# Spectral filter and two-layer MLP in one kernel: first-stage pieces every second tick, transforms done by tick 148, three more blocks by Strassen's scheme

## The chip, the cores and the metric

The kernel runs on one core of a Trainium2 chip. The metric is the device time of one execution, in microseconds (us). Before the change the median of 3 runs is 1342.98 us (1342.41 to 1349.44).

## The reference

Everything is fp32. `x` has 4 batches of 3008 rows of 256; the MLP has 12032 tokens, 256 inputs and 2048 hidden values.

```python
X = np.fft.rfft(x, axis=1)                      # 4 x 1505 x 256
Yr = Xr @ w_r - Xi @ w_i + b_r
Yi = Xr @ w_i + Xi @ w_r + b_i
Yr = sign(Yr) * max(|Yr| - 0.01, 0)             # the same for Yi
x = irfft(Yr + 1j * Yi, n=3008).reshape(12032, 256)
h = x @ w_in                                    # 256 -> 2048
g = h / (1 + exp(-h))
out = g @ w_out                                 # 2048 -> 256
```

## The kernel before

**Precision.** Most products split both factors into a high and a low part of TensorE's faster fp32 format and issue three matmuls: high times high, low times high, high times low. A split is a copy on ScalarE (the high part) and a subtraction on VectorE (the low part).

**The transforms** are matrix products in stages of 47 and 64 points, with the layout between the stages changed by a store to device memory and a load. For batches 1 to 3:
- The *first stage* of batches 2 and 3 comes in 16 *pieces* a batch. `stack_split` splits a piece of the input, `stack_product` multiplies it (two matmuls of 512 columns, lines 287 to 300, one PSUM bank each; ScalarE copies one half of the rows out, VectorE adds it to the other) and stores it; it then asks for the input of the piece after the next one (`x_ahead`, on POOL's queue).
- The *second stage* has 12 units a batch. In a *step* `u3_step(b, u, 0)`, `s2_3` does the second transform of unit u (8 small matmuls in one bank, "s2"), `split_z` splits the shrunk spectrum of unit u-2, and `i1` does the first inverse stage of unit u-3 (6 matmuls, another bank). In a *mix* `u3_step(b, u, 1)`, `mix3` multiplies unit u-1 by the weights (18 matmuls of 256 columns: 6 in a first bank, 12 in a second). ScalarE, POOL and VectorE then add bias and shrink; the VectorE part (`shrink`) is put on the list `deferred`.
- The *last stage* `i2(i, 0)`, `i2(i, 1)`, `i2_ends(i)` makes the 512 tokens of MLP block i, already transposed, in three products; `i2_load` loads what they read.

**The MLP** works on 24 blocks of 512 tokens (the last has 256). A block has 16 *ticks*, one for each 128 hidden values. In an ordinary tick `mlp1` does six matmuls of 512 columns (the first layer) and ScalarE applies the activation; `split_g` splits the result in the next tick; `mlp2` does the second layer of the tick before the last one: four groups of a 512- and a 256-column matmul into four accumulators. Blocks in `FAST` do the first layer by Strassen's scheme: in a pair of ticks, seven products of 2 x 2 blocks instead of eight, 21 matmuls of 256 columns instead of 12 of 512, with more additions on VectorE and POOL, and with sums of the weights (`fast_weights`) and of the tokens (`fast_moving`) made beforehand.

**PSUM.** Of eight banks, four are the second layer's accumulators, two ("h") the first layer's, and two ("d0", "d1") are handed out in turn by `bank(name)` (line 175) to every product of the transforms. A bank is written again only when those that read it are done.

**The order of work** is written out by hand. `ticks` lists (block, f); `fill[t]` holds what a tick t does besides. A loop at the end (lines 1085 to 1119) issues, for each tick: the deferred shrinks, `split_g` of the tick before, `mlp1`, then `fills(t)`, then the second layer with `run`. `fills` ends with `flush`, which issues up to four waiting stores on SP's queue. `put(t, ...)` (line 1002) takes the next tick that is free; ticks 33, 49, 65, ... are kept free, since the outputs of a block are copied out there. Before the change every last-stage product, every piece and every step or mix has a tick of its own, by the strings of "U" (a step or a mix) and "S" (a piece); the transforms end with tick 183, and blocks 13 to 22 are in `FAST`.

Of the kernel before, what the change touches and what calls it, by code (L numbers as in the profile page):

```python
# [9 lines left out]
F32 = mybir.dt.float32  # L10
# [23 lines left out]

STACKED = 2

FAST = range(13, 23)

X_BUFS = [0, 1, 2, 3, 4, 5, 6, 0, 1, 2, 3, 4, 0, 2, 1, 0]
BLOCKS = [(c, min(BLK, NT - c)) for c in range(0, NT, BLK)]  # L40
# [109 lines left out]
def spectral_mlp_kernel(ctx: ExitStack, tc: tile.TileContext, x, w_r, w_i, b_r, b_i, w_in, w_out, c1, c2, c3, c4, c3f, c5, out):  # L150
# [24 lines left out]
    def bank(name):  # L175

        state["d"] += 1
        tag, bufs = f"d{state['d'] % 2}", 1
        if state["prologue"]:
            tag, bufs = ((f"d{state['d'] // 4 % 2}", 1), ("acc", 4), ("h", 2), ("acc", 4))[state["d"] % 4]  # L180
        if state["fast"]:
            tag = "d1"
        return ps.tile([128, 512], F32, tag=tag, bufs=bufs, name=name)
# [10 lines left out]
    def flush(n):  # L194
        for dst, src in stores[:n]:
            nc.sync.dma_start(out=dst, in_=src)
        del stores[:n]
# [280 lines left out]
    def pieces(c0, n):  # L478

        c = c0  # L480
        while c < c0 + n:
            b, q = divmod(c, S)
            v = next(v for v in PLACES[b] if v[0] <= q < v[0] + v[1])
            p0 = q - v[0]
            m = min(v[1] - p0, c0 + n - c)
            yield c - c0, b, v, p0, m
            c += m
# [11 lines left out]
            nc.sync.dma_start(out=t[0:96, q], in_=v[:, j * D:(j + 2) * D])  # L499
            nc.sync.dma_start(out=t[96:120, q], in_=w[h * NR:(h + 1) * NR, c * D:(c + 2) * D])  # L500

    def i2_load(i):
        if i >= len(BLOCKS):
            return
        for _, b, (_, _, kind, k), _, _ in pieces(*BLOCKS[i]):
            g = k // 4 if kind == "pair" else ("five", k[0] // 2)
            if (b, g) not in loaded:
                loaded.add((b, g))
                if kind == "five":
                    f_load(b, g[1])  # L510
                else:
                    g_load(b, g, cols=slice(k % 4 * D, 4 * D))
# [4 lines left out]
    def i2_columns(p, e, b, place):  # L517
# [9 lines left out]
        for h, o in enumerate((0, NP)):  # L527
# [3 lines left out]
                start=(h == 0), stop=(h == 1), skip_group_check=True,  # L531
            )

    def i2(i, e):

        c0, n = BLOCKS[i]
        if e == 0:
            v = "ab"[i > 0] if i < 3 else "ab"[(i + 1) % 2]
            xt[i] = tuple(sb.tile([128, 2, BLK], F32R, tag=f"xt{v}{k}", bufs=1, name=f"xt{k}") for k in range(2))
        whole = [v for v in pieces(c0, n) if v[4] == v[2][1]]  # L540
        p = bank("i2")
        for o, b, place, _, m in whole:
            i2_columns(p[:, o:o + m], e, b, place)
        q = slice(whole[0][0], whole[-1][0] + whole[-1][4])
        if i in FAST and e == 0:
            xf[i] = tl.tile([128, 2, BLK], F32, tag="xf", bufs=1, name="xf")
        split_x(i, p[:, q], (slice(None), e, q))
# [9 lines left out]
    def i2_ends(i):  # L557

        c0, n = BLOCKS[i]
        if i in rest:  # L560
            t = rest.pop(i)
            split_x(i, t, (slice(None), slice(None), slice(0, t.shape[-1])))
        o, b, place, p0, m = list(pieces(c0, n))[-1]
        z = place[1]
        if p0 == 0 and m < z:
            p = bank("i2e").rearrange("p (e c) -> p e c", e=2)[:, :, :z]
            for e in range(2):
                i2_columns(p[:, e, :], e, b, place)
            split_x(i, p[:, :, 0:m], (slice(None), slice(None), slice(o, o + m)))
            rest[i + 1] = sb.tile([128, 2, 216], F32, tag="rest", bufs=1, name="rest")[:, :, 0:z - m]  # L570
            nc.scalar.copy(rest[i + 1], p[:, :, m:z])
# [63 lines left out]
    def fast_moving(i):  # L635

        x32 = xf.pop(i)
        d = tl.tile([128, 4, HB], F32, tag="td", bufs=1, name="td")
        hi = tl.tile([128, 4, HB], F32R, tag="th", bufs=2, name="th")
        lo = tl.tile([128, 4, HB], F32R, tag="tl", bufs=2, name="tl")  # L640
        th[i] = (hi, lo)
        l0, r0, l1, r1 = x32[:, 0, 0:HB], x32[:, 0, HB:BLK], x32[:, 1, 0:HB], x32[:, 1, HB:BLK]

        def low(k):
            nc.gpsimd.tensor_sub(lo[:, k, :], d[:, k, :], hi[:, k, :])

        nc.gpsimd.tensor_sub(d[:, 0, :], r0, l0)
        yield
        nc.gpsimd.tensor_sub(d[:, 1, :], r1, d[:, 0, :])
        yield  # L650
        nc.gpsimd.tensor_sub(d[:, 2, :], r1, r0)
        nc.scalar.copy(hi[:, 0:2, :], d[:, 0:2, :])
        yield
        low(0)
        yield
        nc.gpsimd.tensor_sub(d[:, 3, :], l1, d[:, 1, :])
        yield
        low(1)
        nc.scalar.copy(hi[:, 2:4, :], d[:, 2:4, :])
        yield  # L660
        low(2)
        yield
        low(3)
# [176 lines left out]
    with tc.manual_schedule():  # L840
# [156 lines left out]
        def at(t, fn, *args):  # L997
            fill.setdefault(t, []).append((fn, args))
# [3 lines left out]
        def put(t, fn, *args):  # L1002

            while t in taken:
                t += 1
            taken.add(t)
            at(t, fn, *args)
            return t

        for i in range(1, len(BLOCKS)):  # L1010
            t = (16 * i - 15 if i in FAST else 16 * i - 9) if i > 1 else -1
            if i > 1:
                at(t, i2_load, i)
            put(t + 2, i2, i, 0)
            put(t + 4, i2, i, 1)
            t = put(t + 6, i2_ends, i)
            if i in FAST:
                moving = fast_moving(i)
                for k in range(8):
                    at(t + 1 + k, next, moving, None)  # L1020
                assert t + 8 < 16 * i
        for t, n in enumerate(W_GO):
            at(t, w_go, n)
        at(0, x_ahead)
# [5 lines left out]
        m3 = mix3_weights()  # L1030
        for t in (16, 22, 23):
            at(t, next, m3, None)
        def turns(b):

            for u in range(NU + 3):
                for half in range(2 if 0 < u <= NU else 1):
                    yield b, u, half

        free, stacked = 24, 18
        for b, order in ((1, "U" * 4 + "UUUUSUUUS" * 3 + "UU" + "S." * 10), (2, "UUSUUSUSUS" * 3 + "USUS" + "USU" * 2 + "UUU"), (3, "U" * 27)):  # L1040
            todo, split = list(turns(b)), 0
            assert order.count("U") == len(todo) and order.count("S") in (0, 16)
            ready = max(free, stacked + 4)
            for k in range(2):
                at(ready - 2 + k, u_load, b, k)
            for k in order:
                if k == "U":
                    free = put(max(free, ready), u3_step, *todo.pop(0))
                elif k == "S":
                    while free in taken:  # L1050
                        free += 1
                    at(max(free - 2, stacked), stack_split, b + 1, split)
                    stacked = put(free, stack_product, b + 1, split)
                    split += 1
                last = free
                free += 1

        def swap_pools():
            nonlocal tl
# [4 lines left out]
        for q in range(NFF // 2):  # L1064
            steps = fast_weights(q)
            for k in range(3):
                at(last + 2 + q * 8 // 5 + k, next, steps, None)
        assert last + 1 <= 16 * FAST[0] - 13 and last + 2 + 11 + 2 < 16 * FAST[0] + 12

        def fills(t):  # L1070
            for fn, args in fill.pop(t, []):
                fn(*args)
            flush(1 if t < 12 else 4)

        def run(n):
            for v in units[:n]:
                mlp2(*v)
            del units[:n]
# [5 lines left out]
        first_fast, last_fast = 16 * FAST[0], 16 * (FAST[-1] + 1)  # L1084
        for t in range(len(ticks) + 1):
            i, f = ticks[t] if t < len(ticks) else (LAST, None)
            while deferred:
                deferred.pop(0)()
            if t and ticks[t - 1][0] not in FAST:
                split_g(*ticks[t - 1])  # L1090
            if i in FAST:
                q = t - first_fast
                if f % 2 == 0:
                    state["fast"] = True
                    fast_one(i, f // 2)
                    run(2)
                    if q:
                        fast_two()
                        run(2 if q > 2 else 0)
                else:  # L1100
                    fast_more()
                    if f != 3:
                        rest_of_pair()
                    run(2 if q < 4 else 4)
                    rest_of_pair()
                fills(t)
                continue
            if t == last_fast:
                run(2)
                fast_two()  # L1110
                run(3)
                rest_of_pair()
            if f is not None:
                mlp1(i, f)
            fills(t)
            if last_fast <= t < last_fast + 3:
                run(3 if t == last_fast else 4)
            else:
                run(sum(v[:2] != ticks[t - 1] for v in units))
        run(len(units))  # L1120
        for k, (dst, src) in enumerate(stores):
            eng = nc.scalar if k % 2 else nc.sync
# [28 lines left out]
```

## Time and profile before

| | |
|---|---|
| median of 3 runs | 1342.98 us (1342.41 to 1349.44) |
| profiled execution, its own time | 1344.73 us |
| its span, first to last instruction | 1342.9 us |
| granted TensorE clock, mean over the span | 0.997 |
| busy: TensorE matmuls, weight loads | 1328.4 us (99%), 1176.5 us (88%) |
| busy: VectorE, ScalarE, POOL | 857.0 us (64%), 790.3 us (59%), 191.0 us (14%) |
| DMA | 109.96 MB, mean 82 GB/s |

PE is TensorE's matmuls, PEld its weight loads, DVE VectorE, ACT ScalarE, POOL GpSimd and SP SyncE, which issues most DMAs. L591 is line 591 of the kernel before. Matmuls are pipelined and overlap: one of 512 columns is shown with 0.40 us, while the next starts 0.23 us later, so start to start is the measure of a matmul's cost. In the timeline a bracket at the end of a line gives the idle time before it and what ended it.

### The profile page before, as it was taken

Reading aid. Unit: us, or ns where it says so; the run is one execution under the profiler, and the core shown is the slowest. Engines: PE = TensorE matmul, PEld = TensorE weight load, DVE = VectorE, ACT = ScalarE, POOL = GpSimd, SP = SyncE. Lnnn points to the kernel's source line nnn. Section 1 sums busy time; section 2 is a strip of 40 time slices with the busy share of each in tenths; the row PEclk is TensorE's granted clock in tenths of the full one; section 3 lists DMA queues with packets and bytes.
Section 4 is the critical chain, followed back from the end, with each engine's and each line's share of the span. In section 5 each row is a group of like instructions: output and inputs, shape, how many; then the busy total and the mean of one; then the engine's idle time right before and its main releaser. Section 6 shows DMA issues by size and latency. Waiting matters only on the chain.

```text
span 1342.9 us, 22228 instructions
## 1 busy us (share of the span) xinstructions
PE 1328.4 (99%) x8221; PEld 1176.5 (88%) x8221; DVE 857.0 (64%) x1628; ACT 790.3 (59%) x1646; POOL 191.0 (14%) x292
## 2 busy tenths in 40 slices
PE   8989999999999999999999999999999999999998
PEld 4967888888888888888889888899999999999998
DVE  3867747675665757676556557366666666666663
ACT  5546555565676666575555455466656665666555
POOL 2000002111111212120111100211112111211100
PEclk9999999999999999999999999999999999999999
DMA  8875514342345345251424121011001110110000
GB/s 274 261 214 172 151 40 113 95 116 67 101 105 149 93 111 147 70 144 36 141 64 125 53 77 30 2 32 31 16 23 31 31 30 3 31 32 13 4 22 25
DMA packets 76121, 109.96 MB, mean 82 GB/s; under 512 B 8854, under 2 KB 54798, under 8 KB 76014
## 3 DMA queue, kind: packets, MB, share of 16 engines
q1 hardware_dynamic: 61895, 79.17, 20.5%
q0 software_dynamic: 10544, 25.68, 7.4%
q10 hardware_dynamic: 3575, 3.70, 0.9%
q8 instruction: 65, 1.06, 0.3%
q14 instruction: 42, 0.34, 0.1%
HBM read 71.03 MB, written 37.49 MB: 81 GB/s over the span
## 4 chain that ended last, share of the span: by engine, by line
PE 95%; DMA 4%; ACT 1%; DVE 0%; SPq 0%; issue 0%; ACTq 0%; DVEq 0%
PE acc L749 25%; PE h L591 22%; PE h L672 15%; PE acc L753 13%; PE mix L415 6%; PE s L390 2%; PE i L462 2%; PE mix L354 2%; PE i2e L529 2%; PE i L529 2%; PE s L293 1%; DMA scr<-i1o 1%; DMA scr<-s1o 1%; PE acc L744 1%; PE i L459 1%; PE i L522 1%
## 5 line engine op out<-in xcount | busy, mean ns | idle before, releaser
L749 PE MATMUL acc<-wout,gh 128*128 128x512 f32 x1472 | 541.3, 398 | 0.6 <-ACT gh L607 0.6
L753 PE MATMUL acc<-wout,gl 128*128 128x256 f32 x1472 | 413.5, 281 | 0.2 <-DVE gl L608 0.2
L591 PE MATMUL h<-xt,win 128*128 128x512 f32 (+1 forms) x1344 | 339.2, 387 | 0.0
L749 PEld LDWEIGHTS acc<-wout,gh 128*128 128x128 f32 x1472 | 277.9, 189 | 50.1 <-ACT gh L607 0.8
L598 ACT ACTIVATE g<-h 128x512 f32<-128x512 f32 (+2 forms) x225 | 130.9, 582 | 267.4 <-PE h L591 265.3
L753 PEld LDWEIGHTS acc<-wout,gl 128*128 128x128 f32 x1472 | 277.1, 188 | 5.0 <-DVE gl L608 0.5
L591 PEld LDWEIGHTS h<-xt,win 128*128 128x128 f32 x1344 | 232.2, 188 | 48.1 <-DVE xt L555 0.4
L608 DVE TENSOR_TENSOR gl<-g,gh 128x512 fp32r<-128x512 f32 (+2 forms) x225 | 151.2, 674 | 75.8 <-ACT gh L607 73.2
L607 ACT CAST gh<-g 128x512 fp32r<-128x512 f32 (+2 forms) x225 | 136.1, 606 | 1.5
L720 DVE TENSOR_TENSOR gl<-gp,gh 128x512 fp32r<-128x512 f32 x160 | 113.7, 711 | 24.4 <-ACT gh L719 24.4
L710 ACT ACTIVATE gp<-gp 128x256 f32<-128x256 f32 x80 | 33.4, 417 | 135.6 <-DVE gp L707 135.6
L719 ACT CAST gh<-gp 128x512 fp32r<-128x512 f32 x160 | 99.3, 621 | 5.2
L434 DVE TENSOR_TENSOR y<-q,mix 64x256 f32<-64x256 f32 x144 | 60.3, 419 | 59.1 <-PE mix L415 56.8
L422 POOL TENSOR_TENSOR q<-q,bias 128x256 f32<-128x256 f32 x36 | 26.5, 737 | 405.9 <-ACT q L421 405.9
L672 PE MATMUL h<-xt,win 128*128 128x256 f32 x480 | 83.8, 283 | 0.2 <-DVE gp L707 0.2
L712 DVE TENSOR_TENSOR gp<-h,u 128x256 f32<-128x256 f32 x80 | 33.9, 424 | 60.7 <-ACT gp L711 60.7
L672 PEld LDWEIGHTS h<-xt,win 128*128 128x128 f32 x480 | 68.2, 189 | 3.8 <-DVE gp L707 0.4
L672 PE MATMUL h<-th,sw_h 128*128 128x256 f32 x240 | 70.2, 293 | 0.0
L672 PE MATMUL h<-th,sw_l 128*128 128x256 f32 x240 | 68.0, 283 | 0.0
L672 PE MATMUL h<-tl,sw_h 128*128 128x256 f32 x240 | 67.4, 281 | 0.0
L295 DVE TENSOR_TENSOR s1o<-s,s1o 48x512 f32<-48x512 f32 x64 | 41.0, 678 | 32.3 <-ACT s1o L294 32.2
L707 DVE TENSOR_TENSOR gp<-h,u 128x256 f32<-128x256 f32 x80 | 33.8, 423 | 42.7 <-PE h L672 42.4
(175 smaller groups left out, 2260.0 us busy)
## 6 DMA issues: line engine op xcount, KB each, us to landing
a<-scr SPq DMA_DIRECT2D x48, 256.0 KB
x_sb<-in_x_dram POOLq DMA_DIRECT2D x64, 188.0 KB, 3.7
gin<-scr SPq DMA_DIRECT2D x48, 192.0 KB
t<-in_c_dram POOLq DMA_DIRECT2D x36, 256.0 KB, 3.2
scr<-i1o SPq DMA_DIRECT2D x36, 256.0 KB
t<-in_c_dram SPq DMA_DIRECT2D x48, 128.0 KB
scr<-s1o SPq DMA_DIRECT2D x32, 192.0 KB
scr<-s1o SPq DMA_DIRECT2D x13, 384.0 KB
```

The costliest lines, as they stand in the source:

```text
L415: nc.tensor.matmul(out=out, lhsT=x_[:, e, c, :], rhs=m[:, e, :], start=(n == 0), stop=(n == 5))
L434: nc.vector.tensor_tensor(out=y[64 * i:64 * i + 64, r, :], in0=q[rows, i, :], in1=pv[rows, i, :], op=op,)
L529: nc.tensor.matmul(out=p[:, o:o + NP + RR], lhsT=t[:, q:q + 128], rhs=c4_sb[:, h * (NP + RR):(h + 1) * (NP + RR)], start=(h == 0), stop=(h ...
L591: nc.tensor.matmul(out=p[:, :n], lhsT=w[:, e, f * 128:(f + 1) * 128], rhs=v[:, e, :n], start=(m == 0), stop=(m == 5),)
L598: nc.scalar.activation(out=g[:, q], in_=p[:, q], func=ACTF.Silu)
L607: nc.scalar.copy(gh[:, q], g[:, q])
L608: nc.vector.tensor_sub(gl[:, q], g[:, q], gh[:, q])
L672: nc.tensor.matmul(out=p, lhsT=w[j], rhs=m[k], start=(begins and n == 0), stop=(n == 2), skip_group_check=True,)
L719: nc.scalar.copy(h, v)
L720: nc.vector.tensor_sub(l, v, h)
L749: nc.tensor.matmul(out=a, lhsT=gh[:, q], rhs=wout[:, f].rearrange("p a c -> p (a c)"), start=begins, stop=False,)
L753: nc.tensor.matmul(out=a[:, D:2 * D], lhsT=gl[:, q], rhs=wout[:, f, 0, :], start=False, stop=ends,)
```

## The change

`FAST` begins at block 10 instead of 13. The planner of ticks is new:
- Pieces are placed first, at least two ticks apart; steps and mixes take the other ticks, in order. A last-stage product of blocks 3 to 9 no longer has a tick of its own: it joins a tick with a mix or a piece (or, when its time is up, any), at least two ticks after the last one.
- Keys of `fill` may be fractions. `fills(t - 0.25)` and `fills(t - 0.125)` come before the tick's `mlp1`, `fills(t + 0.5)` after its second layer. A mix is put at t - 0.125. A last-stage product that joins a mix or a step is put at t + 0.5; a piece that a last-stage product joins is itself put at t + 0.5, and the split of the next piece at t + 0.75.
- The deferred shrinks are issued after `mlp1` of the mix's own tick, no longer at the start of the next one. `flush` runs in the whole ticks only.
- The last stage takes an "h" bank (`stage_bank`), except in the opening and while Strassen blocks run.
- The load of a batch's first group of columns waits for the third of a block's products (`late`).
- The steps end with tick 148. The weight sums then take ticks 150 to 163, and block 10, the first of `FAST`, starts at tick 160.

The diff, without the parts that only pass `late` on:

```diff
-FAST = range(13, 23)
+FAST = range(10, 23)
...
+    def stage_bank(name):
+
+        if state["prologue"] or state["fast"]:
+            return bank(name)
+        return ps.tile([128, 512], F32, tag="h", bufs=2, name=name)
...
-        p = bank("i2")
+        p = stage_bank("i2")
...
-            p = bank("i2e").rearrange("p (e c) -> p e c", e=2)[:, :, :z]
+            p = stage_bank("i2e").rearrange("p (e c) -> p e c", e=2)[:, :, :z]
...
+        steps = []
+        for b in range(1, NB):
             for u in range(NU + 3):
-                for half in range(2 if 0 < u <= NU else 1):
-                    yield b, u, half
-
-        free, stacked = 24, 18
-        for b, order in ((1, "U" * 4 + "UUUUSUUUS" * 3 + "UU" + "S." * 10), (2, "UUSUUSUSUS" * 3 + "USUS" + "USU" * 2 + "UUU"), (3, "U" * 27)):
...
+                steps.extend((b, u, half) for half in range(2 if 0 < u <= NU else 1))
+        pieces_left = [(b, q) for b in range(STACKED, NB) for q in range(16)]
+        turned = []
+        for i in range(3, FAST[0]):
+            at(16 * i - 15, i2_load, i)
+            begins = any(v[1] and v[2][0] == 0 for v in pieces(*BLOCKS[i]))
+            turned.extend((16 * i - (3 if k == 2 and begins else 13), 16 * i - 7 + 2 * k, fn)
+                          for k, fn in enumerate(((i2, i, 0), (i2, i, 1), (i2_ends, i))))
+        stacked, last, begun = {1: 18}, 24, set()
+        ended = {}
+        done, behind, t, since = 37, False, 24, 0
+        while steps or turned:
+            boundary = t % NFF == 1 and t > 32
+            stage = None
+            if not boundary and t not in taken:
+                b = steps[0][0] if steps else NB
+                ready = b in stacked and t >= stacked[b] + (4 if b > 1 else 0)
+                apart = 2 + (ready and b > 1 and len(pieces_left) % 2)
+                if pieces_left and t >= done + apart and pieces_left[0][0] <= b + 1:
+                    stage = "piece"
+                elif ready:
+                    stage = "mix" if steps[0][2] else "step"
+            more = None
+            if turned and t >= turned[0][0] and t >= since + 2 and not (boundary and t < turned[0][1]):
+                if stage in ("mix", "piece", None) or t >= turned[0][1]:
+                    more = turned.pop(0)[2]
+                    since = t
+            if stage == "piece":
+                at(done + 0.75 if behind else max(t - 2, done), stack_split, *pieces_left[0])
+                at(t + 0.5 * (more is not None), stack_product, *pieces_left[0])
+                done, behind = t, more is not None
+                if pieces_left.pop(0)[1] == 15:
+                    stacked[max(stacked) + 1] = t
+            elif stage:
...
+                at(t - 0.125 * steps[0][2], u3_step, *steps.pop(0))
+                last = t
+                ended[b] = t
+            if more:
+                at(t + 0.5 * (stage in ("mix", "step")), *more)
...
-            flush(1 if t < 12 else 4)
+            if t == int(t):
+                flush(1 if t < 12 else 4)
...
-            while deferred:
-                deferred.pop(0)()
             if t and ticks[t - 1][0] not in FAST:
                 split_g(*ticks[t - 1])
+            fills(t - 0.25)
+            fills(t - 0.125)
...
             if f is not None:
                 mlp1(i, f)
+            while deferred:
+                deferred.pop(0)()
             fills(t)
             if last_fast <= t < last_fast + 3:
                 run(3 if t == last_fast else 4)
             else:
                 run(sum(v[:2] != ticks[t - 1] for v in units))
+            fills(t + 0.5)
```

## Rows read from the trace of the kernel before

**Rows 1.** The page's first part: busy us, share of the span, instructions.
```profile
PE 1328.4 (99%) x8221; PEld 1176.5 (88%) x8221; DVE 857.0 (64%) x1628; ACT 790.3 (59%) x1646; POOL 191.0 (14%) x292
```

**Rows 2.** The page's fourth part: the chain that ended last, shares by engine.
```profile
PE 95%; DMA 4%; ACT 1%; DVE 0%; SPq 0%; issue 0%; ACTq 0%; DVEq 0%
```

**Rows 3.** Waits of TensorE, 131 to 1339 us: total us, times, longest us.
```profile
PE h L672 <- DVE gp L707: 0.2, 1, 0.2
PEld h L672 <- DVE gp L707: 0.4, 1, 0.4
...
PEld acc L749 <- DVE o L772: 0.2, 1, 0.2
```

**Rows 4.** Windows: length, busy us of each engine, clock, DMA share, GB/s.
```profile
206.60:273.30 66.70, 66.70 (x407) 59.26 (x406) 45.82 (x87) 37.90 (x78) 13.91 (x22) 1.00 0.38 104
...
822.18:868.98 46.80, 46.80 (x243) 39.58 (x242) 22.19 (x46) 25.34 (x52) 7.39 (x8) 1.00 0.08 23
912.67:956.99 44.32, 44.32 (x315) 41.53 (x313) 30.27 (x62) 27.84 (x63) 7.32 (x10) 1.00 0.09 24
```

**Rows 5.** The chain in order of time: start us, us, what; a mix, a first layer.
```profile
199.55 2.15 PE mix L415 x18
203.10 1.40 PE h L591 x6
```

**Rows 6.** Timeline of a step, tick 162: start us, us, engine, line, operation.
```profile
705.15 1.05 PE L390 MATMUL s<-t,a 128*128 128x128 f32 x8
...
706.75 0.40 PE L749 MATMUL acc<-wout,gh 128*128 128x512 f32 x1
...
707.47 0.68 DVE L402 TENSOR_TENSOR xl<-s,xh 128x512 fp32r<-128x512 f32 x1
...
708.15 1.56 PE L591 MATMUL h<-xt,win 128*128 128x512 f32 x6
708.42 0.58 ACT L466 COPY i1o<-i 128x512 f32<-128x512 f32 x1
```

**Rows 7.** Timeline of a piece, tick 80.
```profile
394.83 0.63 PE L293 MATMUL s<-sx,c_sb 111*128 111x512 f32 x2
395.03 0.60 ACT L598 ACTIVATE g<-h 128x512 f32<-128x512 f32 x1 [1.54 <-PE h L591]
...
395.30 0.39 PE L749 MATMUL acc<-wout,gh 128*128 128x512 f32 x1
...
395.66 1.07 ACT L294 COPY s1o<-s 48x512 f32<-48x512 f32 x2
...
396.28 0.68 DVE L295 TENSOR_TENSOR s1o<-s,s1o 48x512 f32<-48x512 f32 x1 [2.06 <-ACT s1o L294]
```

**Rows 8.** Groups by line, the pieces' own: count, busy us, mean ns, idle before.
```profile
L295 DVE TENSOR_TENSOR s1o<-s,s1o 48x512 f32<-48x512 f32 x64 | 41.0, 678 | 32.3 <-ACT s1o L294 32.2
...
L294 ACT COPY s1o<-s 48x512 f32<-48x512 f32 x64 | 34.2, 583 | 2.7 <-DMA scr<-s1o 1.9
...
L293 PE MATMUL s<-sx,c_sb 111*128 111x512 f32 x64 | 20.2, 396 | 0.0
```

**Rows 9.** Timeline of the opening stage: two transform products close together.
```profile
30.56 0.59 ACT L339 CAST xh<-s 128x512 fp32r<-128x512 f32 x1 [1.98 <-PE s L333]
...
31.25 1.13 PE L333 MATMUL s<-t,a 128*128 128x128 f32 x8 [0.73 <-ACT xh L339]
```

**Rows 10.** Timeline of tick 3.
```profile
114.99 0.58 PE L522 MATMUL i<-c_sb,gin 96*128 96x94 f32 x4
...
116.57 0.59 ACT L598 ACTIVATE g<-h 128x512 f32<-128x512 f32 x1
...
116.72 0.49 PE L749 MATMUL acc<-wout,gh 128*128 128x512 f32 x1 [0.64 <-ACT gh L607]
```

More of the change, by code (lines that the diff above doesn't have):

```diff
@@ L500, in f_load, with i2_load @@
             nc.sync.dma_start(out=t[96:120, q], in_=w[h * NR:(h + 1) * NR, c * D:(c + 2) * D])
-    def i2_load(i):
+    def i2_load(i, late=False):
         if i >= len(BLOCKS):
             return
-        for _, b, (_, _, kind, k), _, _ in pieces(*BLOCKS[i]):
+        for _, b, (o, _, kind, k), _, _ in pieces(*BLOCKS[i]):
+            if b and o == 0 and not late:
+                continue
             g = k // 4 if kind == "pair" else ("five", k[0] // 2)
@@ L1008, in put, with last_stage @@
             return t
[L1010 to L1021, printed above, removed]
+        def last_stage(i, first):
+            at(first - 2, i2_load, i)
+            put(first, i2, i, 0)
+            put(first + 2, i2, i, 1)
+            at(first + 2, i2_load, i, True)
+            return put(first + 4, i2_ends, i)
+        for k, fn in enumerate(((i2, 1, 0), (i2, 1, 1), (i2_ends, 1))):
+            put(1 + 2 * k, *fn)
+        last_stage(2, 25)
         for t, n in enumerate(W_GO):
@@ new lines, in spectral_mlp_kernel @@
+        done, behind, t, since = 37, False, 24, 0
[22 more added lines that the diff above has]
+            elif stage:
+                if b not in begun:
+                    begun.add(b)
+                    for k in range(2):
+                        at(t - 2 + k, u_load, b, k)
+                at(t - 0.125 * steps[0][2], u3_step, *steps.pop(0))
[3 more added lines that the diff above has]
+                at(t + 0.5 * (stage in ("mix", "step")), *more)
+                if more[0] is i2_ends:
+                    at(t - 2, i2_load, more[1], True)
+            t += 1
@@ new lines, in spectral_mlp_kernel @@
+        assert ended[1] < 16 * 5 - 5 and ended[2] < 16 * 11 - 15 and ended[3] < 16 * 17 - 15
+        assert all(16 * i > t for t, v in fill.items() for fn, (i, *_) in [(v[0][0], v[0][1] or (99,))] if fn is i2_ends)
+        for i in range(FAST[0], len(BLOCKS)):
+            if i in FAST:
+                first = max(16 * i - 13, last + 1)
+                t = last_stage(i, first)
+                moving = fast_moving(i)
+                for k in range(8):
+                    at(t + 1 + (k if first == 16 * i - 13 else k // 2), next, moving, None)
+                assert t + 8 < 16 * i or first > 16 * i - 13
+            else:
+                last_stage(i, 16 * i - 7)
@@ L1067, in spectral_mlp_kernel @@
                 at(last + 2 + q * 8 // 5 + k, next, steps, None)
-        assert last + 1 <= 16 * FAST[0] - 13 and last + 2 + 11 + 2 < 16 * FAST[0] + 12
+        assert last + 1 <= 16 * FAST[0] - 11 and last + 2 + 11 + 2 < 16 * FAST[0] + 12
         def fills(t):
```

17 lines of the change are left out of this document (removed).

## The prediction

> **What bounds the kernel now.** I read the page's busy times first: TensorE has matmuls running in 1328.4 us of a 1342.9 us span [rows 1]. As ends of matmuls are modelled, I checked this with the chain of waits, which puts 95% of the span on TensorE and 4% on DMA [rows 2]; the DMA part lies before tick 0, which starts at about 105 us. The third view is the waits of TensorE alone. From 131 us to the end its matmuls wait once, for 0.2 us, and its weight loads four times, for 1.1 us in all [rows 3]. So for nine tenths of the span the order of instructions on TensorE is the time: whatever is taken off TensorE is gained in full, and whatever makes it wait is paid in full. No other engine is near its limit: in the densest transform stage VectorE is busy 45.82 us of 66.70 [rows 4].
>
> **Part 1: blocks 10, 11 and 12 by Strassen's scheme.** The windows of single blocks give the price without a model. Block 12, ordinary, with the last transform stage of block 13 in it and no step of the transforms, runs from 822.18 to 868.98: 46.80 us. Block 14, by the scheme, with the same kind of last stage in it, takes 44.32 us [rows 4]. Both are gapless on TensorE. The difference, 2.48 us a block, is gained three times: **-7.44 us**. What the scheme adds on other engines lies beside TensorE: VectorE 30.27 and ScalarE 27.84 us of 44.32 [rows 4].
>
> Here a rule speaks against the change. The rows give 1.40 us for the six 512-column matmuls of an ordinary tick, 0.234 us each [rows 5]; a pair of ticks has 12 of them, the scheme 21 of 256 columns. The Trainium skill (TensorE: Matmul & The Clock Gate, section Back-to-back issue gap) gives a sustained 131 ns at 512 columns and 81 ns at 128; between them about 98 ns at 256, an estimate from that page. By it a pair would go from 1.57 to 2.06 us and three blocks would lose 11.7 us instead of gaining 7.44. The ten blocks that already run so contradict it.
>
> **Part 2: transforms in ticks 24 to 148 instead of 24 to 183.** Nothing is added here: the same steps, mixes, 32 first-stage pieces and last-stage products are issued. What changes is who stands next to whom on TensorE. Before, all of a tick's transform products stood after the tick's first layer, so that the four second-layer products (1.40 us, 706.75 to 708.15 [rows 6]) and mostly the next first layer (1.40 us) lay between two users of the two PSUM banks d0 and d1. Now a mix stands ahead of its tick's first layer, and a piece that shares its tick with a last-stage product stands behind the second layer. The bank counter goes on by two in a piece (one bank for each half), by two in a mix, by one in a step's s2 and one in its i1. So a mix always begins on the bank of the piece's first half, or of the s2, before it. Stepping through the planner's loop gives three kinds of neighbours.
>
> (a) A piece half a tick late, and a mix directly behind it: pieces at ticks 39, 52, 56, 70, 77, 100 and 103, mixes at 40, 53, 57, 71, 78, 101 and 104. **Seven times**. (The late pieces at 54 and 105 have a step behind them, and a first layer between.) The mix could start 0.47 us after the piece's first matmul (394.83 to 395.30) [rows 7]. Its bank is free after that matmul (0.396), the copy of half a piece (0.583) and the addition (0.678) [rows 8]: 1.66 without any hand-over, 1.70 with about 0.02 at each. TensorE resumes some 0.1 us after the release: where two such products stood together in the opening stage, the copy ended at 31.15 and the next matmul came at 31.25, after 0.73 us of waiting [rows 9]. So 1.70 + 0.10 - 0.47 = 1.33 us each, **+9.3 us**. Lower bound 1.19 (durations alone), upper 1.76: the release at 2.13 after the first matmul (394.83 to 396.96 [rows 7]), with the activation of the same tick ahead of the copy. I take the lower part, as that activation is long done when the piece comes half a tick later.
>
> (b) A piece in its normal place and a mix at the next tick: 43, 47, 60, 66, 82, 89, 92, 110, 114. **Nine times**. Here the second layer lies between: the mix could start at 0.47 + 1.40 = 1.87, the bank comes free at 2.13 [rows 7], TensorE resumes at 2.23: 0.35 each, **+3.2 us**. Bounds: 0 (if the copy came first, 1.70) and 1.05 (one more subtraction of 0.7 us in VectorE's queue).
>
> (c) A step and a mix at the next tick: 14 times with s2 and i1 in the step (34, 36, 85, 95, 106, and nine from 125 to 142), three times with s2 alone (31, 121, 123). From s2's first matmul at 705.15 the second layer ends at 708.15, 3.00 us; the last reader of s2's bank ends at 707.47 + 0.68 = 708.15 too, so 0.1 for resuming. The mix's second bank is wanted 0.72 us on (6 of 18 matmuls in 2.15 us [rows 5]), at 3.82, and is i1's, whose copy ends at 709.00, 3.85, plus 0.1: another 0.13 [rows 6]. 0.23 times 14, and 0.15 times three: **+3.7 us**. Bounds 0 and 0.9 each (a queue of one subtraction more; at tick 106, a piece's split lies ahead of the step).
>
> In (a) to (c) the waiting instruction is a mix's matmul; all of TensorE's work stands behind it (its own rest, the first layer, the second), so each wait is paid in full, and nobody gives it back.
>
> **Part 3: the last stage on the first layer's banks.** The product takes one of the two h banks; the first layer two ticks on takes it next, at least 1.40 + 1.40 us later, against a copy and a subtraction of the size of a piece's (1.26 us [rows 8]). I cost it at nothing, with one exception: ticks 1 to 5, where ScalarE is held by the conversion of the weights. There, in tick 3, the product at 114.99 would now wait for the activation that ends at 116.57 + 0.59 = 117.16; the second layer behind it waited anyway (0.64 us, to 116.72) [rows 10]. That is +0.9 us there, part of which small waits up to 131 us give back: I take **+0.5**, bounds -0.5 and +1.2.
>
> **What else moves, at nothing.** The subtractions of the shrink come after the first layer instead of at the next tick's start: the gl that now precedes them is wanted two ticks on. Pieces every second tick: so they stood at ticks 80 to 88 before, gapless [rows 7]; the steps now between them lengthen two ticks and so the time for their loads on POOL's queue. Stores go out at whole ticks only, so a late piece's leaves one tick later, behind what SP already holds; its readers come four ticks later. Closest is batch 1's end: last i1 at tick 73, late load on SP at 75, its product at 77, with 13 us of TensorE's work between (four ticks of 2.8, two s2 and a piece). Weight sums up to tick 163 overlap the first fast ticks on VectorE. I take 0 for both, with 0 to 3 us as bounds.
>
> **Sum.** -7.44 + 9.3 + 3.2 + 3.7 + 0.5 = +9.2 us. The profiled execution took 1344.73 (span 1342.9 and 1.83 around it), so it would be 1353.9; the median of the runs, 1342.98, lies 1.75 below, which gives **1352.2 us**. With (a) between 8.3 and 12.3, the sum's own range is 1348 to 1358.
>
> **Rivals.**
> - *Only the half-tick neighbours wait.* If ScalarE copies a piece ahead of the activation, (b) goes, and (c) lies at the edge of its 3.00 us anyway. Then -7.44 + 9.3 = +1.9: 1345. For it: (c)'s margins are hundredths of a us; against: the activation was ahead in the rows [rows 7].
> - *The other side: the banks come free in time.* Place: the seven late pieces and the mixes. It is not slower if all waits together are under 7.44 us, which, with (b) and (c) at nothing, means under 1.06 us at each of the seven; at no waits the time is 1335.5. For it: no product after 131 us waits for a bank now [rows 3]. Against: none stood so close, and the copy and addition alone take 1.26 us [rows 8]. A wait of that kind did hold TensorE in the opening stage [rows 9].
> - *The queues of VectorE and ScalarE fall behind.* Ticks 39 to 117 hold pieces, steps and mixes together; VectorE, busy 69% in the densest stage before [rows 4], would be at some 80% there, an estimate from 125 ticks for what 160 held. At the upper bound of (a), 0.7 at (b) and 0.6 at (c): 12.3 + 6.3 + 10.2 - 7.44 = +21: 1364. For it: VectorE works in order; against: the results of a tick are wanted two ticks later, 2.8 us of slack.
> - *The scheme itself loses.* It does where a 256-column product costs over 2 x 1.40 / 21 = 0.134 us [rows 5]; at two thirds of 0.234, 0.156, a block would lose 8 x (21 x 0.156 - 2.80) = 3.8 us, and three with the waits 11.4 + 16.7: 1371. The measured blocks, 2.48 us shorter, exclude it all but wholly [rows 4]. This is the case that the page's rule above describes.
>
> **How the numbers follow.** The forecast 0.58, the first rival 0.20, the other side 0.08, queues 0.13, the rule 0.01. What a measurement of this kernel can tell is 0.5%, 6.7 us: slower means over 1349.7, faster under 1336.3. Of the forecast's 0.58 about 0.10 lies under 1349.7. Slower 0.48 + 0.13 + 0.01 = 0.62, same 0.30, faster 0.08. For 8 in 10 the range takes in the first rival and the lower part of the queues' case: 1342 to 1360; the forecast's own is 1348 to 1358.
>
> **What would show it.** Waits of TensorE's weight loads or matmuls in the mix, ended by VectorE's addition of a piece: seven of about 1.3 us and nine of about 0.3; ended by the subtraction after s2 or the copy of i1: some 17, around 0.2. Blocks 10 to 12 at 44.3 us. If the waits ended by that addition come to less than 4 us, or blocks 10 to 12 are not shorter by 2.4 us than an ordinary one, the working is wrong.

## The result, and the profile after

The changed kernel takes **1358.47 us** (median of 6 runs, 1357.59 to 1364.09) against 1342.83 for the kernel before (median of 6 runs that alternated with them): a ratio of 1.0107, 95% interval 1.0081 to 1.0134. It is slower by 1.1%: 14.4 us by the ratio, 15.6 by the medians. The forecast was 1352.2, with a range of 1342 to 1360; its direction and its mechanism were right, its sum 6 us short. The profiled execution took 1358.72 us, with a span of 1356.8.

The page of the profile after, its busy times and its chain of waits (these answer to [rows 1] and [rows 2]):

```profile
PE 1328.0 (98%) x8437; PEld 1182.8 (87%) x8437; DVE 909.4 (67%) x1742; ACT 812.5 (60%) x1712; POOL 226.1 (17%) x322
...
PE 90%; DMA 3%; DVE 3%; ACT 2%; issue 1%; SPq 0%; DVEq 0%; ACTq 0%
```

TensorE is busy as long as before (1328.0 against 1328.4 us) in a span 13.9 us longer. In the profile the added time is idle time of TensorE. (The busy time has not fallen by the 7.44 us that the scheme takes off, in part because matmuls behind a wait and at the lower clock are shown longer, as rows below have it.) 5% of the chain has passed from TensorE to VectorE, ScalarE and issue. The waits say where. First those of TensorE's matmuls, then those of its weight loads, from 131 us to the end (they answer to [rows 3], which had no wait over 0.4 us):

```profile
PE mix L415 <- DVE s1o L295: 8.4, 8, 1.2
PE h L680 <- DVE gp L715: 2.2, 1, 2.2
PE mix L415 <- DVE xl L402: 0.5, 1, 0.5
```

```profile
PEld mix L415 <- DVE s1o L295: 15.4, 16, 1.6
PEld mix L415 <- ACT xh L401: 4.4, 14, 0.8
PEld h L680 <- DVE gp L715: 2.4, 1, 2.4
PEld mix L415 <- issue: 0.5, 3, 0.2
...
```

The 16 waits for a piece's addition (L295) are the seven and the nine of the prediction; the 14 below are its 14 steps with two banks (the one for L402 is among them, at tick 106), and the three by "issue" are its three steps with s2 alone. The line of L680, at the first block by Strassen's scheme, is in no term of the prediction's sum.

The windows of blocks 9 to 12 after (they answer to the two blocks in [rows 4]; columns as there):

```profile
694.29:746.40 52.11, 52.11 (x287) 44.73 (x285) 34.64 (x69) 29.20 (x60) 10.32 (x10) 1.00 0.13 39
746.40:792.59 46.19, 44.02 (x302) 41.20 (x301) 33.90 (x75) 26.90 (x62) 6.05 (x8) 0.96 0.12 34
792.59:836.90 44.31, 44.31 (x314) 41.54 (x313) 29.76 (x62) 27.74 (x63) 7.57 (x10) 1.00 0.09 24
836.90:881.21 44.31, 44.31 (x314) 41.53 (x313) 29.82 (x62) 27.66 (x63) 7.66 (x10) 1.00 0.09 24
```

Blocks 11 and 12 take the 44.3 us that were forecast, gapless. Block 10 has 2.17 us of idle TensorE in it, and its mean clock is 0.96.

A late piece and the mix behind it, tick 39 to 40 (timeline; it answers to [rows 7]):

```profile
242.87 0.62 PE L293 MATMUL s<-sx,c_sb 111*128 111x512 f32 x2
243.31 1.06 ACT L294 COPY s1o<-s 48x512 f32<-48x512 f32 x2 [0.46 <-PE s L293]
243.92 1.28 DVE L295 TENSOR_TENSOR s1o<-s,s1o 48x512 f32<-48x512 f32 x2 [1.45 <-ACT s1o L294]
244.66 0.51 PE L415 MATMUL mix<-wr,xh 128*128 128x256 f32 x2 [1.16 <-DVE s1o L295]
245.00 0.28 PE L415 MATMUL mix<-wr,xl 128*128 128x256 f32 x1
245.12 0.40 PE L415 MATMUL mix<-wr,xh 128*128 128x256 f32 x2
245.36 0.28 PE L415 MATMUL mix<-wr,xl 128*128 128x256 f32 x1
```

The copy starts at 243.31, on ScalarE that is free, the addition of the first half at 243.92; it ends some 0.6 later, and the mix begins at 244.66: 1.79 us after the piece's first matmul, where it could have stood at 0.47. That is a wait of 1.32. The rows also show something that the prediction lacks: the first two matmuls of the mix take 0.34 us from start to start (244.66 to 245.00), the next two 0.24 (245.12 to 245.36). Behind a wait, the second matmul comes 0.1 us late (0.07 in the steps below).

A step and the mix behind it, ticks 126 to 127 (timeline; it answers to [rows 6]):

```profile
628.71 0.68 DVE L402 TENSOR_TENSOR xl<-s,xh 128x512 fp32r<-128x512 f32 x1
629.27 0.28 PE L761 MATMUL acc<-wout,gl 128*128 128x256 f32 x1
629.50 0.30 PEld L415 LDWEIGHTS mix<-wr,xh 128*128 128x128 f32 x2 [0.27 <-ACT xh L401]
629.53 0.47 PE L415 MATMUL mix<-wr,xh 128*128 128x256 f32 x2
629.66 0.58 ACT L466 COPY i1o<-i 128x512 f32<-128x512 f32 x1
...
630.32 0.47 PE L415 MATMUL mix<-wi,xh 128*128 128x256 f32 x2
```

The mix starts 0.26 us after the last second-layer matmul instead of 0.12, and 0.14 after the subtraction L402, the last reader of s2's bank, ended (629.39). The profile names L401, a cast that ended earlier, at 629.23. But the mix multiplies the unit before this step's and does not read that cast's result (`u3_step` gives `mix3` unit u-1); experiment 5 decides between the two in the times as well. The second bank, wanted at the seventh matmul, is held by the copy of i1 to 630.24, and the pair at 630.32 is stretched (0.47 instead of 0.40).

### The profile page after: what moved, and what is told of

It is laid out like the page before. It is cut to its first block, busy times and chain, and to the rows that moved or that the text cites. A ratio compares the mean times of both kernels' runs of the same rounds, so it can differ in the third digit from the quotient of the medians.

```text
span 1356.8 us, 22826 instructions
## 1 busy us (share of the span) xinstructions
PE 1328.0 (98%) x8437; PEld 1182.8 (87%) x8437; DVE 909.4 (67%) x1742; ACT 812.5 (60%) x1712; POOL 226.1 (17%) x322
## 4 chain that ended last, share of the span: by engine, by line
PE 90%; DMA 3%; DVE 3%; ACT 2%; issue 1%; SPq 0%; DVEq 0%; ACTq 0%
PE acc L757 24%; PE h L680 19%; PE h L599 16%; PE acc L761 12%; PE mix L415 6%; PE s L390 2%; PE i L462 2%; PE mix L354 2%; PE i2e L531 2%; PE i L531 2%; PE s L257 1%; DMA scr<-i1o 1%; PE acc L752 1%; DVE s1o L295 1%; ACT s1o L294 1%
## 5 line engine op out<-in xcount | busy, mean ns | idle before, releaser
L599 PE MATMUL h<-xt,win 128*128 128x512 f32 (+1 forms) x1056 | 264.8, 386 | 0.0
L606 ACT ACTIVATE g<-h 128x512 f32<-128x512 f32 (+1 forms) x177 | 101.9, 576 | 192.7 <-PE h L599 191.3
L599 PEld LDWEIGHTS h<-xt,win 128*128 128x128 f32 x1056 | 181.6, 188 | 34.5 <-DVE xt L563 0.4
L728 DVE TENSOR_TENSOR gl<-gp,gh 128x512 fp32r<-128x512 f32 x208 | 148.5, 714 | 31.7 <-ACT gh L727 31.6
L616 DVE TENSOR_TENSOR gl<-g,gh 128x512 fp32r<-128x512 f32 (+1 forms) x177 | 120.1, 679 | 48.8 <-ACT gh L615 46.8
L727 ACT CAST gh<-gp 128x512 fp32r<-128x512 f32 x208 | 129.0, 620 | 6.6
L680 PE MATMUL h<-xt,win 128*128 128x256 f32 x624 | 109.1, 284 | 2.2 <-DVE gp L715 2.2
L615 ACT CAST gh<-g 128x512 fp32r<-128x512 f32 (+1 forms) x177 | 106.1, 600 | 1.7
L680 PEld LDWEIGHTS h<-xt,win 128*128 128x128 f32 x624 | 88.7, 189 | 6.8 <-DVE gp L715 2.4
L680 PE MATMUL h<-th,sw_h 128*128 128x256 f32 x312 | 91.6, 294 | 0.0
L680 PE MATMUL h<-th,sw_l 128*128 128x256 f32 x312 | 88.5, 284 | 0.0
L680 PE MATMUL h<-tl,sw_h 128*128 128x256 f32 x312 | 87.8, 281 | 0.0
L715 DVE TENSOR_TENSOR gp<-h,u 128x256 f32<-128x256 f32 x104 | 44.1, 424 | 55.5 <-PE h L680 55.2
L434 DVE TENSOR_TENSOR y<-q,mix 64x256 f32<-64x256 f32 x144 | 60.3, 419 | 25.1 <-POOL q L422 14.5
L726 ACT ACTIVATE gp<-gp 128x512 f32<-128x512 f32 x104 | 66.4, 638 | 0.0
```

The costliest lines, as they stand in the source:

```text
L434: nc.vector.tensor_tensor(out=y[64 * i:64 * i + 64, r, :], in0=q[rows, i, :], in1=pv[rows, i, :], op=op,)
L599: nc.tensor.matmul(out=p[:, :n], lhsT=w[:, e, f * 128:(f + 1) * 128], rhs=v[:, e, :n], start=(m == 0), stop=(m == 5),)
L606: nc.scalar.activation(out=g[:, q], in_=p[:, q], func=ACTF.Silu)
L615: nc.scalar.copy(gh[:, q], g[:, q])
L616: nc.vector.tensor_sub(gl[:, q], g[:, q], gh[:, q])
L680: nc.tensor.matmul(out=p, lhsT=w[j], rhs=m[k], start=(begins and n == 0), stop=(n == 2), skip_group_check=True,)
```

## The experiments

The theory (T) was: the loss is the hand-over of the two d banks from a piece or a step to the mix directly behind it. Rivals: VectorE, ScalarE or the transfers are simply too full with the transforms packed into 125 ticks; or the loss lies in the blocks by Strassen's scheme. The runs of the kernel before that alternated with them had medians of 1343.03 us (experiments 1 to 4) and 1344.68 us (5 to 8), so kernels are compared by their ratios.

**1. The mix behind its tick's first layer**, as every step is, in all three batches.

```diff
-                at(t - 0.125 * steps[0][2], u3_step, *steps.pop(0))
+                at(t, u3_step, *steps.pop(0))
```

> Undoes one part: every mix is issued behind its tick's first layer again; all else as changed. Theory (banks): the mixes' waits are for the two transform banks and for nothing else, so all of them (about 19 us with the 0.1 us that the weight loads lose after each wait) go, and no other wait takes their place: 1358.5 - 19 = 1339.5 us, between 1337.5 and 1342. Rival (queues): VectorE and ScalarE are behind in the denser ticks, the mixes only show it; then the waits move to the second layer or the next step and at most half is gained: 1349 or more.

Measured: 1368.75 us, ratio 1.019 (1.0173 to 1.0207). A miss: slower than the change, not faster. The waits of the mix did go, but others came in their place. Waits of matmuls over the whole run:

```profile
PE s L293 <- DVE y L434: 8.4, 4, 2.7
PE i L462 <- issue: 7.0, 5, 2.2
```

L434 is the shrink, which reads the mix's second bank. One of the four in the timeline:

```profile
360.06 0.47 ACT L559 CAST xt<-i 128x376 fp32r<-128x376 f32 x1 [3.27 <-PE i L524]
360.56 0.55 DVE L563 TENSOR_TENSOR xt<-i,xt 128x376 fp32r<-128x376 f32 x1 [3.58 <-ACT xt L559]
...
361.28 0.40 PE L293 MATMUL s<-sx,c_sb 111*128 111x512 f32 x1
361.79 1.72 DVE L434 TENSOR_TENSOR y<-q,mix 64x256 f32<-64x256 f32 x4
...
363.65 0.47 PE L293 MATMUL s<-sx,c_sb 111*128 111x512 f32 x1 [1.97 <-DVE y L434]
```

With the mix moved, the loop reaches the list of shrinks before the mix has put its own on it; the shrink is issued only in the next tick, behind a last-stage subtraction (L563) for which VectorE itself stands idle 3.58 us. The second half of the piece waits for the bank meanwhile. The five waits of i1 (the second line) have the same end: in each, i1's first matmul starts 0.10 us after the last of the shrink's four additions (L434), which read the bank that i1 takes. It is still the hand-over of a bank, from the other side, and the edit as I made it did not tell T from its rivals. Behind this wait TensorE's clock fell too (window of 3.4 us; the clock is the third figure from the end):

```profile
364.96:368.36 3.40, 3.40 (x11) 2.72 (x10) 2.96 (x4) 1.25 (x2) 1.01 (x2) 0.51 0.41 102
```

**2. No late pieces**: a piece that a last-stage product joins stays in its place before the second layer.

```diff
-                at(t + 0.5 * (more is not None), stack_product, *pieces_left[0])
+                at(t, stack_product, *pieces_left[0])
```

> Undoes another part alone: a piece that shares its tick with a last-stage product is issued in the whole tick, ahead of that product and of the second layer, so that 2.3 us of other products lie between it and the mix. Theory (banks): the seven waits of 1.31 us, 9.9 us with the loads' refill after them, go and the waits of the other neighbours stay as they are: 1348.6 us (1347 to 1350.5). Rival (queues): VectorE has the same work in the same ticks, so the time stays at 1357 to 1359.

Measured: 1347.81 us, ratio 1.0049 (1.0034 to 1.0065), as T has it. Waits of weight loads from 131 us:

```profile
PEld mix L415 <- DVE s1o L295: 4.4, 9, 0.7
PEld mix L415 <- ACT xh L401: 4.2, 14, 0.6
```

Seven of the 16 waits for L295 are gone, the nine and the 14 stand. The seven alone were worth 0.58% (1.0107 to 1.0049), 7.8 us, by the ratios, and 10.7 by the traces, counted from the first tick to the end (see "The sum" below); 9.9 was expected.

**3. Block 1's last stage on the d banks**, so that in ticks 1 to 5 it has not to wait for the activation.

```diff
-        p = stage_bank("i2")
+        p = bank("i2") if i == 1 else stage_bank("i2")
```

(the same for "i2e").

> The last stage of block 1 alone (ticks 1 to 5) takes the transform banks again. Theory: the two waits of TensorE for an activation in ticks 1 and 3 (0.87 and 1.93 us in the trace) go, but the second layer of tick 3 then waits for ScalarE as before the change, so 1.0 us is gained: 1357.5. Rival: the arrival of the weights sets these ticks whatever the bank, nothing is gained.

Measured: 1358.0 us, ratio 1.0111 (1.0091 to 1.0131): too small a part for the time to show. The waits of matmuls in the first ticks do, first of the change, then of this kernel:

```profile
PE i L524 <- ACT g L606: 2.8, 2, 1.9
```

```profile
PE i L531 <- DMA gin<-scr: 0.6, 1, 0.6
PE acc L757 <- ACT gh L615: 0.5, 1, 0.5
...
```

The last stage no longer waits for the activation. Laid tick on tick against the kernel before, ticks 0 to 5 are 1.02 us longer in the change and 0.07 shorter here; from the first tick to the end this kernel is 1.05 us shorter than the change.

**4. The weight sums earlier**: eight pairs in steps of one tick, so that they end before block 10.

```diff
-                at(last + 2 + q * 8 // 5 + k, next, steps, None)
+                at(last + 2 + q + k, next, steps, None)
```

> The sums of the weights for Strassen's scheme start one every tick instead of five in eight ticks, so that the last is begun at tick 157 and not at 161, in the first Strassen block. Theory: the wait of 2.17 us at tick 162, for an addition on VectorE that stands behind the last weight sums, and the small ones after it go: block 10 takes 42.7 us instead of 46.2, and the whole 1355. Rival (queues): VectorE, with 2.6 us of sums in each tick of 2.8, only falls behind earlier and makes the second layer wait in ticks 152 to 160: 1357 to 1360.

Measured: 1359.43 us, ratio 1.0114 (1.009 to 1.0138): no gain, as the rival has it. Blocks 9 and 10 of this kernel, and the new wait of its matmuls:

```profile
697.51:751.80 54.29, 52.70 (x287) 44.48 (x286) 38.75 (x81) 30.14 (x62) 9.46 (x10) 1.00 0.12 38
751.80:794.69 42.89, 42.70 (x302) 39.73 (x301) 29.39 (x62) 25.29 (x59) 6.04 (x8) 1.00 0.13 36
```

```profile
PE acc L761 <- DVE gl L616: 1.6, 2, 1.2
```

Block 10 is 3.30 us shorter than in the change, block 9 is 2.18 longer: the denser sums now make the split of the ordinary ticks late. Together they are 1.1 us shorter, less than the times can show. The cost is VectorE's queue in this place; most of it only moved to other ticks.

**5. The mix begins on the other bank**: one more step of the bank counter ahead of each mix, nothing else.

```diff
+        state["d"] += 1
         p = bank("mix")
```

> As changed, but the bank counter is moved on by one ahead of every mix, so that a mix begins on the bank of the piece's second half (or of i1) and takes the first half's bank second. Nothing moves on any engine. Theory (banks): the wait is for whichever bank the mix takes first, and those come free later: the second addition some 0.6 us after the first (seven late pieces: +4.3; nine pieces in whole ticks: +5.8), the copy of i1 0.8 us after the subtraction of s2, less the second wait that then goes (14 steps: +9): 1358.5 + 19 = 1377 us, between 1371 and 1382. Rival (the mix waits for its operands, or the queues are behind): which bank comes first is all one, 1357 to 1360.

Measured: 1387.42 us, ratio 1.032 (1.0299 to 1.0342). Where the order, the engines' loads and the transfers stay as they are and only the bank differs, the rivals have no reason for a change of time. Waits of weight loads from 131 us:

```profile
PEld mix L415 <- DVE s1o L295: 25.0, 16, 2.2
PEld mix L415 <- ACT i1o L467: 15.4, 14, 1.6
PEld mix L415 <- ACT xh L401: 2.9, 3, 1.0
```

The same 16 and 14 waits, each for the reader of the bank that came later: a piece's second half, and behind a step the copy of i1 instead of the reader of s2's bank. The three below are the steps with s2 alone, where the mix now begins on s2's bank. From start to start, a wait behind a late piece grew from 1.55 to 2.15 us, behind a whole-tick piece from 0.42 to 1.02: 0.60 each, where the addition of a second half takes 0.68 [rows 8]. It also settles what the 14 waits are: they go by the bank, not by the cast that the profile named. The time went some 5 us beyond the range expected: after four of the seven longest waits the clock was halved for 3.4 us (granted 0.50 to 0.51), and the three steps with s2 alone, which the expectation left out, cost 2.2 us more than in the change.

**6. Strassen's scheme from block 13**, as before, with all else of the change.

```diff
-FAST = range(10, 23)
+FAST = range(13, 23)
```

> The new order alone: blocks 10 to 12 ordinary, the transforms still done by tick 148. Theory: three times 2.48 us are lost again, and the 3.5 us that the late weight sums cost in the first Strassen block are gained, since that block now starts 45 ticks after them: 1358.5 + 7.4 - 3.5 = 1362.4 us, and the whole difference to the kernel before, 19.5, is the new order's. Rival: the scheme in blocks 10 to 12 is itself part of the loss; then this is under 1358.

Measured: 1362.12 us, ratio 1.0132 (1.0118 to 1.0146). Block 12 of this kernel, and block 13, its first by the scheme:

```profile
839.06:885.85 46.79, 46.79 (x242) 39.56 (x241) 14.88 (x24) 23.50 (x48) 7.40 (x8) 1.00 0.08 22
885.85:929.54 43.69, 43.50 (x311) 40.76 (x309) 28.91 (x61) 25.16 (x59) 5.87 (x8) 1.00 0.09 25
```

By the ratios the three blocks give the change some 0.25% (1.0132 to 1.0107), 3.4 us, of the 7.44 that three blocks save; the two intervals overlap, so that the times alone do not settle it. The traces do: from the first second-layer matmul of block 9 to that of block 14 it is 236.27 us here (703.31 to 939.58) and 232.49 in the change (704.14 to 936.63), 3.8 us less. The entry into the scheme takes the rest.

**7. The mix behind the first layer and its shrink right behind the mix**: experiment 1 without its flaw.

```diff
-                at(t - 0.125 * steps[0][2], u3_step, *steps.pop(0))
+                at(t, u3_step, *steps.pop(0))
...
             if f is not None:
                 mlp1(i, f)
+            fills(t)
             while deferred:
                 deferred.pop(0)()
-            fills(t)
```

> The mix behind its tick's first layer, as in x1_mix_after, and its shrink issued right behind it, ahead of the last-stage product that shares its tick. In x1 that product's subtraction stood ahead of the shrink on VectorE and held the mix's second bank. Theory (banks): with the banks free in time no product of the transforms waits; what is left of the new waits is 3.5 us at the first Strassen block and 1.0 in ticks 1 to 5: 1358.5 - 19 = 1339.5 us (1337.5 to 1342), faster than before by 3.4. Rival (queues): the dense ticks need more than VectorE has, and waits of pieces or second layers of over 5 us in all stay: over 1345.

Measured: 1340.49 us, ratio 0.9979 (0.9964 to 0.9993). Of the waits of matmuls from 131 us on, one is left:

```profile
PE h L680 <- DVE gp L715: 2.2, 1, 2.2
```

All of the change's work is in this kernel, packed into the same ticks; only the mix and its shrink have moved by one first layer. It takes 1.3% less than the change. With experiment 5 this excludes the full engines and the transfers as the cause of the mixes' waits.

**8. The same, with the two smaller losses mended**: experiment 7, block 1's last stage as in experiment 3, and the scheme from block 11, sixteen ticks later, so that the sums are done before it.

```diff
-FAST = range(10, 23)
+FAST = range(11, 23)
```

> z1_mix_and_shrink_after with block 1's last stage on the transform banks and Strassen's scheme from block 11, so that the weight sums end 13 ticks before the first Strassen block. Theory: no new wait is left; two blocks at 2.48 us are gained against the kernel before: 1343.0 - 5.0 = 1338.0 us (1336.5 to 1340). Rival (queues): as above, over 1343.

Measured: 1339.17 us, ratio 0.9966 (0.9951 to 0.998): faster than the kernel before by a third of a per cent, and than the change by 1.4%. Its waits of matmuls from 131 us on, and its block 11, the first by the scheme (block 10, ordinary, took 46.75):

```profile
PE h L680 <- DVE gp L715: 0.2, 1, 0.2
```

```profile
770.19:813.10 42.91, 42.72 (x302) 39.73 (x301) 28.78 (x61) 24.90 (x59) 6.14 (x8) 1.00 0.09 25
```

TensorE is gapless again, as it was before the change, and two blocks by the scheme are the net gain. A version with the sums paced for an entry at block 10 was not tried on the chip.

## Why the prediction was right, and where it was short

**Part 1 (-7.44): right.** Blocks 11 and 12 take 44.31 us, an ordinary one of the same kernel with the scheme from 13 takes 46.79 (experiment 6). The rule of the Trainium skill that the prediction set against this (TensorE: Matmul & The Clock Gate, section Back-to-back issue gap) is contradicted once more: by the estimate that the prediction made from it these blocks would have been longer than ordinary ones, and they are 2.5 us shorter.

**Part 2, the waits for the banks (+16.2): right in kind, place and number; measured +19.0.** These sums are worked out from the starts of the matmuls around all mixes in the trace of the change.

| | predicted | measured |
|---|---|---|
| (a) late pieces | 7 x 1.33 = 9.3 | 7 x 1.31 = 9.2, and 7 x 0.10 behind the waits: 9.9 |
| (b) pieces at whole ticks | 9 x 0.35 = 3.2 | 8 x 0.30 + 0.51 = 2.9, and 9 x 0.11: 3.9 |
| (c) steps | 14 x 0.23 + 3 x 0.15 = 3.7 | 4.6 + 3 x 0.21 = 5.2 |

The step that was short is the price of one wait: I ended it where TensorE resumes. The matmul after that one comes 0.1 us late as well (244.66 to 245.00 above), and in (c) 0.07 us is paid twice, once for each bank; tick 106, where a piece's split lay ahead of the step, has a wait of 0.66, within the upper bound given. In (a) and (b) the choice of the lower part of the bounds was right: the copy of a late piece found ScalarE free. The hand-overs from engine to engine, put at 0.02 each without a row, took 0.03 to 0.04 in the late piece above (matmul to copy, copy to addition).

In one place a wrong premise was covered by luck. The prediction says that a mix always begins on the bank of the piece's first half, or of the s2, before it. Behind a step with s2 alone the counter has moved on by one only, so the mix begins on the other bank and wants s2's at its seventh matmul, where the trace has the wait: 0.21 us each against 0.15. On s2's bank at once it would have been far more: in experiment 5, where the mix does begin there, it is 0.93 us each. The prediction names no row for its 0.15.

**Part 3 (+0.5): right in kind, measured +1.0.** The last stage waited for the activation in ticks 1 to 5 as described, twice instead of once; the second layer behind it gave back less than I took. The 1.0 is that of one execution. Six other kernels have the same work in these ticks, and there ticks 0 to 5 were 0.45 to 2.64 us longer than before; in the three highest (experiments 4, 6 and 7: 2.35 to 2.64) the clock fell to 0.50 for 3.4 us behind this wait.

**"What else moves, at nothing": wrong in one place, +3.5 us.** The weight sums were costed at 0 with 3 as a bound. The entry into the scheme, VectorE and TensorE in the timeline of the change:

```profile
750.64 0.68 DVE L640 TENSOR_TENSOR sw_l<-wd,sw_h 128x512 fp32r<-128x512 f32 x1
...
752.70 0.28 DVE L634 TENSOR_TENSOR wd<-wf,wd 128x128 f32<-128x128 f32 x1
752.90 0.75 DVE L780 TENSOR_TENSOR o<-acc,o 128x256 f32<-128x256 f32 x2
753.57 0.42 DVE L715 TENSOR_TENSOR gp<-h,u 128x256 f32<-128x256 f32 x1
754.03 0.81 PE L680 MATMUL h<-xt,win 128*128 128x256 f32 x3 [2.17 <-DVE gp L715]
```

```profile
754.30:757.70 3.40, 3.40 (x16) 3.20 (x16) 2.50 (x6) 3.09 (x8) 0.00 (x0) 0.50 0.26 49
```

VectorE has no idle time in these rows. The addition that frees a bank of the scheme's products (L715) stands in its queue behind six instructions of the weight sums and the output's additions, nearly 3 us of work, and starts at 753.57; TensorE waits 2.17 us and then runs 3.4 us at half clock. Against the 42.71 us of the same entry in experiment 8 (42.91 less its wait of 0.2), block 10 costs 3.5 more: 2.17 of wait and 1.3 that the matmuls run longer (44.02 against 42.72 busy). So 3.5 of the 7.44 saved are given back at once; by the traces of experiment 6 it is 3.7. The rival of the queues had the right cause, VectorE's order, but sought it at the pieces; there it didn't occur. This term should have had its own check: how long VectorE's queue is in the first ticks of the scheme.

**The sum.** -7.44 + 19.0 + 1.0 + 3.5 = +16.1 against +9.2 predicted. From the first tick to the end the profiled execution of the change is 15.1 us longer than that before, so the terms come to 1.0 us too much, and where that lies is open; its span is only 13.9 longer, as the opening, up to the first matmul of the first layer, took 104.26 us instead of 105.46. The change does not touch the opening, and in the other kernels here, which have the same, it took from 100.8 us (experiment 8) to 106.5 (experiment 1): a spread that is in every time given above. Counted from the first tick to the end, against the kernel before, experiment 2 is 4.3 us longer, experiment 7 is 1.6 shorter and experiment 8 is 5.2 shorter, where its two blocks by the scheme and ticks 0 to 5 give 5.1. Of the 6 us by which the forecast was short, 3.5 are the entry into the scheme and 2.8 the waits for the banks, most of it the 0.1 us behind each; both had been taken as free, the first with 3 us as a bound.

## What to carry to other kernels

Where one engine is gapless, a new order is priced by its neighbours: list each pair of users of the same buffer that becomes adjacent, subtract what stands between them from the reader's chain, and add what the pipeline needs to fill again. Work that is nobody's bottleneck, like the weight sums, still sets the time of the instruction behind it in its queue; look at that queue at the one tick where a result first becomes urgent. And when an order is mended, move the readers together with the writer: the mix alone cost 0.8% more (ratio 1.019 against 1.0107), the mix with its shrink 1.3% less (0.9979).

## What the runs showed of the hardware that was not expected

- **The clock after a wait.** After some of the waits in which TensorE's matmuls were idle for 1.68 to 2.7 us, its granted clock fell to 0.50 or 0.51, its lower level (1.2 GHz), for 3.4 us. It did so at the entry into the scheme in the change (754.30) and in experiments 2, 3, 5 and 7, and did not in experiment 1, with the same wait of 2.2 us. In experiment 1 it fell behind the four waits for the shrink (1.89 to 2.68 us) and not behind the one of 2.24 for i1; in experiment 5 behind four of seven of 1.75 us; in tick 3 behind waits of 1.68 to 1.85 us in experiments 4, 6 and 7, and not behind 1.93 us in the change. So the same wait can have it or not. Behind the late pieces of the change, with 1.15 to 1.16 us of idle TensorE each by the profile (less than the 1.32 worked out above, as the modelled end of the matmul before lies late), it stayed at 1.00, and in experiment 8 its mean was 1.000. A long wait can thus cost well over its length (1.3 us more in block 10), and the seven short ones, 8.1 us in all, did not. A window of the change that holds a late piece, its wait and the mix:

```profile
242.00:251.00 9.00, 7.84 (x46) 6.61 (x46) 6.73 (x13) 4.51 (x9) 3.64 (x5) 1.00 0.24 59
```

- **VectorE beside POOL.** A subtraction of 128 x 512 with both operands in SBUF took 1.23 us while POOL was at work on its own subtractions, and 0.68 with POOL idle (750.64 above; the window 742 to 754 has POOL at 0.00). The Trainium skill (SBUF — State Buffer, section Who interferes with whom) says that a VectorE instruction with two SBUF inputs contends with a GpSimd one that reads SBUF; the rows agree:

```profile
737.80 1.23 DVE L640 TENSOR_TENSOR sw_l<-wd,sw_h 128x512 fp32r<-128x512 f32 x1
```

```profile
737.29 3.48 POOL L653 TENSOR_TENSOR tl<-td,th 128x256 fp32r<-128x256 f32 x3
```

Whether this has a part in VectorE's queue being behind at the entry into the scheme was not tried, and the rows do not show it: between the two VectorE stood idle for 0.61 us, up to 742.86, waiting for a copy on ScalarE.
